# A retention layer with two feed-forward layers in float32: the gate in turns without a clamp pass, and the retention's decays moved from the output to query, state copy, key and mask

## The chip, the cores and the metric

The kernel runs as one program on one core of a Trainium2 chip. The metric is the device time of a run in microseconds. Three runs of the kernel before took 1521.79, 1521.57 and 1521.58 us; the median is 1521.58. The engines are named as in the profile: PE multiplies matrices into eight PSUM banks, DVE and ACT do elementwise work from and to SBUF and PSUM, POOL does elementwise work in SBUF, and SP does nothing here but issue DMAs. Each engine takes its instructions in the order in which the program hands them over, and waits where an operand is not there yet.

## The reference, cut to what matters

```python
gamma = 1.0 - 2.0 ** (-5.0 - np.arange(H))            # one per head, 8 heads
rel = pos[:, None] - pos[None, :]                     # 576 positions
Dmat = np.where(rel >= 0, gamma[:, None, None] ** rel, 0.0)
x = ((q @ k.T) / sqrt(64) * Dmat) @ v                 # retention; q, k, v: (8, 8, 576, 64)
x = x.transpose(0, 2, 1, 3).reshape(4608, 512)
h = x @ w_in                                          # 512 -> 2048
g = h * np.cos(h)                                     # the gate
x = g @ w_out                                         # 2048 -> 512
h = max(x @ w1, x @ w2, x @ w3)                       # 512 -> 768, three times
out = h @ w_out2                                      # 768 -> 512
```

## The kernel before

**Tiling and products.** The 4608 tokens are nine blocks of 512. Every matrix product is computed in 2x2 quarters by a scheme with seven products in place of eight, and each number is held as a high and a low part, so that one product is three matmuls per slice: low weight by high operand, high by high, high by low. `x_x`, `x_y`, `x_z` and `x_g` are such operands (high parts made by ACT, L360, low parts by DVE, L364), `w_wi` and so on the weights.

**Phases.** From about 0 to 80 us a lead-in splits the first weights and runs the first retention units. From 80 to about 375 us, phase A, the products by two of the four weight groups of w_in run for all blocks, between the retention's matmuls. From there to 573 us, phase B, the other two groups run on operands that are loaded again from DRAM. Then follow the phases wo (w_out), b (w1, w2, w3) and o (w_out2).

**The retention.** One unit is one block and one pair of heads: 36 units. A unit's load brings query, key transposed, key and value into one tile `u` (one DMA, L486). POOL scales the values by gamma to the minus position (`att_scale`, L492). PE computes scores (L504) into two banks `sc`, DVE multiplies them by a causal mask of ones and zeros on the way to SBUF (L513). A running state in PSUM takes key times value per chunk (L547); ACT copies it (L531) ahead of each chunk that follows. PE sums scores by values and query by the state copy into a bank `po` (L563, L575). DVE evacuates `po` chunk by chunk, by a column factor and a row factor (`att_decay`, L590), into the quarters `k_x` from which the operands of the first layer are made. A unit has four chunks of 128 tokens, or three and two of 64.

**The gate.** `group_in` (L405) makes the seven products of one weight group for one block into banks d, b and a; ACT copies and DVE adds (L410) evacuate them into `s_a`. The half tiles of 128x1024 then go through `gate` (L443): ACT takes the number of turns (s over 2 pi plus a quarter, as an integer, L448), DVE subtracts it (rest, L452), a clamp bounds the rest (L453; on POOL in phase A, on DVE in phase B), ACT takes the cosine (L457), DVE multiplies (times, L460), and SP stores the half in DRAM for phase wo (L466).

**What sets the order.** The order is written out by an agenda: `at(n, fn)` puts a piece of work n slots ahead, and `tick()`, called after every product (12 matmuls), hands over what is due. In `gate` the steps stand at `first`, `first + 1`, `first + gap` and so on, `gap` is 3. In `att_unit` the scores stand at `start`, the masks at `start + 1`, the output at `start + 5`, the decay at `start + 6`. All DMAs are issued by SP in one order, so that a store that waits for its gate holds back the loads behind it. Tiles come from a pool of 22 of 4 KB per partition and eight of 14 KB.

Of the kernel before, what the change touches and what calls it, by code (L numbers as in the profile page):

```python
# [20 lines left out]
NB = 512  # L21
# [12 lines left out]
HALF_PI = math.pi / 2.0  # L34
R_LEAST = -0.75
R_MOST = 0.25
WSCALE = 256.0
# [64 lines left out]
def retention_ffn(ctx: ExitStack, tc: tile.TileContext, att, w_in, w_out, w123, w_out2, cst, out):  # L102
# [293 lines left out]
    def last_product(own_slot=True):  # L396

        g = pending.pop()
        product_in(g["d"], g["ws"], P_A22, g["xs"], False)
        nc.scalar.copy(g["s1"][:, 0], g["d"][:, : g["n"]])  # L400
        g["done"](g, 1)
        if own_slot:
            tick()

    def group_in(ws, xs, name, done, where):  # L405
        n = HB * len(ws)
        g = {"ws": ws, "xs": xs, "name": name, "n": n, "done": done, "at": where}
# [9 lines left out]
        s0 = g["s0"] = x4(f"s0_{name}", [2, n])  # L417
        nc.scalar.copy(s0[:, 0], d[:, :n])  # L418
# [4 lines left out]
        nc.scalar.copy(s1[:, 1], b[:, :n])  # L423
        tick()
# [17 lines left out]

    def gate(s, name, dst, first, gap, eng):  # L443
# [75 lines left out]

    def att_keep(n, i):  # L520
# [57 lines left out]

    def att_decay(n):
        u = units.pop(n)  # L580
        j, hp = order_of(n)
        o = quarters_of.setdefault(j, {"name": f"x{j}", "n": NB})
        half = f"k{hp // 2 + 1}"
        if half not in o:
            o[half] = x4(f"{half}_x{j}", [2, NB])
        for _, m, c, pos in chunks_of(j):
            t, cc = divmod(c, HB)
            g = CGS + hp * 9 + pos // 64
            at_ = (hp % 2) * HB + cc
            nc.vector.scalar_tensor_tensor(  # L590
                out=o[half][:, t, at_ : at_ + m],
                in0=u["po"][:, c : c + m],
                scalar=cs[:, g : g + 1],
                in1=cs[:, CG + hp * CH : CG + hp * CH + m],
                op0=ALU.mult,
                op1=ALU.mult,
            )

    def att_unit(n, start):

        at(max(0, start - 1), lambda: att_scale(n))
        at(start, lambda: att_scores(n))
        at(start, lambda: att_keep(n, 0))
# [323 lines left out]
    for j in range(NBLK):  # L927
        for k, ids in enumerate(B_GROUPS):
# [65 lines left out]
```

## Time and profile before

| | |
|---|---|
| median of three runs | 1521.58 us |
| span of the profiled execution | 1516.2 us |
| PE busy | 1454.9 us, 96% |
| DVE busy | 1224.6 us, 81%, 1759 instructions |
| ACT busy | 726.8 us, 48%, 1214 instructions |
| POOL busy | 268.7 us, 18%, 216 instructions |
| moved by DMA | 324 MB, mean 214 GB/s |

A profile is one execution. Its span ends earlier than the measured time begins and ends, by 5.4 us against the median. The busy shares are means over stages that differ; the rows below cut the span by stage.

### The profile page before, as it was taken

To read this page: it belongs to the slowest core of one execution; us is meant where nothing else is said; L and a number is where in the kernel's file an instruction comes from. 1 tells how busy PE (TensorE), PEld (TensorE's weight loads), DVE (VectorE), ACT (ScalarE), POOL (GpSimd) and SP (SyncE) were. 2 spreads that over 40 slices of the span, in tenths; PEclk is the share of its full clock that TensorE was granted. 3 is DMA by queue.
4 is the path that set the end of the run, shared out by engine and by line. 5 is a ranking of instruction groups with operands and counts; after the bars stand their busy time and mean duration, and the time that the engine had idled before them with its cause. 6 is when DMAs were issued, how large, how long until landed. Compare 5 with 4: busy or idle time off the path is not lost.

```text
span 1516.2 us, 30767 instructions
## 1 busy us (share of the span) xinstructions
PE 1454.9 (96%) x12506; PEld 1416.0 (93%) x12506; DVE 1224.6 (81%) x1759; ACT 726.8 (48%) x1214; POOL 268.7 (18%) x216
## 2 busy tenths in 40 slices
PE   6899999999899997899999999999999999999998
PEld 5798989998889997899999999999999999999998
DVE  6888999989889989999999998656664555538997
ACT  3555555556667755454445444334432333323332
POOL 3344444444222001100000000000000000004221
PEclk9899999999999998999999999999999999999999
DMA  7588888876989984556555568923431110254443
GB/s 292 181 292 304 309 300 301 318 290 240 355 304 364 328 294 156 184 193 215 193 203 195 196 216 323 397 107 119 147 127 48 70 66 34 70 191 163 168 168 138
DMA packets 83084, 324.46 MB, mean 214 GB/s; under 512 B 9216, under 2 KB 9216, under 8 KB 76928
## 3 DMA queue, kind: packets, MB, share of 16 engines
q1 hardware_dynamic: 82944, 322.51, 59.4%
q8 instruction: 98, 1.61, 0.4%
q14 instruction: 42, 0.34, 0.1%
HBM read 190.35 MB, written 132.12 MB: 213 GB/s over the span
## 4 chain that ended last, share of the span: by engine, by line
PE 46%; DVE 6%; issue 3%; DMA 2%; ACT 1%; POOL 0%; DVEq 0%; SPq 0%; ACTq 0%; POOLq 0%
PE wo L795 17%; PE d_b L385 14%; PE b_b L385 7%; PE o L795 4%; PE a_b L385 3%; DVE l_m L768 1%; DMA st_o<-p_o 1%; DVE tb_m L356 1%; DVE o_o L808 1%; DVE x_m L759 1%; DVE u_o L808 1%; DMA raw_b<-w 1%; DVE l_g L768 0%; DMA k_m<-mq 0%; ACT h_m L763 0%
## 5 line engine op out<-in xcount | busy, mean ns | idle before, releaser
L795 PE MATMUL wo<-h_g,w_wo 128*128 128x256 f32 x1728 | 314.9, 284 | 0.0
L795 PEld LDWEIGHTS wo<-h_g,w_wo 128*128 128x128 f32 x1728 | 271.3, 193 | 0.0
L795 PE MATMUL wo<-l_g,w_wo 128*128 128x256 f32 x864 | 246.6, 285 | 7.6 <-DVE l_g L768 7.6
L385 PE MATMUL d_b<-x_z,w_b 128*128 128x256 f32 x1944 | 248.8, 283 | 2.9 <-ACT s_b L430 2.1
L385 PEld LDWEIGHTS d_b<-x_z,w_b 128*128 128x128 f32 x1944 | 239.9, 192 | 3.7 <-ACT s_b L430 2.7
L795 PEld LDWEIGHTS wo<-l_g,w_wo 128*128 128x128 f32 x864 | 166.7, 193 | 9.6 <-DVE l_g L768 9.5
L385 PE MATMUL b_b<-x_z,w_b 128*128 128x256 f32 x972 | 131.6, 283 | 2.0 <-DVE x_z L364 2.0
L385 PE MATMUL d_a<-x_x,w_wi 128*128 128x256 f32 x864 | 123.2, 293 | 4.1 <-DVE x_x L364 2.9
L385 PEld LDWEIGHTS b_b<-x_z,w_b 128*128 128x128 f32 x972 | 123.2, 192 | 2.2 <-DVE x_z L364 2.2
L385 PE MATMUL d_a<-x_y,w_wi 128*128 128x256 f32 x864 | 115.3, 291 | 9.2 <-ACT s_a L418 5.8
L385 PEld LDWEIGHTS d_a<-x_y,w_wi 128*128 128x128 f32 x864 | 110.9, 199 | 10.4 <-ACT s_a L418 6.5
L385 PEld LDWEIGHTS d_a<-x_x,w_wi 128*128 128x128 f32 x864 | 110.2, 195 | 8.9 <-DVE x_x L364 4.1
L795 PE MATMUL o<-h_m,w_o 128*128 128x256 f32 x648 | 117.5, 283 | 0.0
L763 ACT CAST h_g<-tb_g 128x1024 fp32r<-128x1024 f32 x36 | 37.8, 1051 | 150.5 <-DVE tb_g L356 145.9
L795 PEld LDWEIGHTS o<-h_m,w_o 128*128 128x128 f32 x648 | 101.1, 192 | 0.0
L452 DVE SCALAR_TENSOR_TENSOR t_a<-s_a,t_a 128x1024 f32<-128x1024 f32 x72 | 99.8, 1389 | 1.4 <-ACT t_a L448 1.4
L410 DVE TENSOR_TENSOR s_b<-s_b,b_b 128x512 f32<-128x512 f32 (+1 forms) x45 | 28.5, 634 | 87.1 <-PE b_b L385 87.0
L460 DVE TENSOR_TENSOR s_a<-s_a,t_a 128x1024 f32<-128x1024 f32 x72 | 90.6, 1274 | 5.9 <-ACT t_a L457 5.9
L457 ACT ACTIVATE t_a<-t_a 128x1024 f32<-128x1024 f32 x72 | 76.3, 1062 | 34.8 <-DVE t_a L453 25.6
L410 DVE TENSOR_TENSOR s_b<-s_b,a_b 128x512 f32<-128x512 f32 (+1 forms) x45 | 28.5, 634 | 79.2 <-PE a_b L385 69.4
L795 PE MATMUL o<-l_m,w_o 128*128 128x256 f32 x324 | 91.8, 283 | 0.0
L418 ACT COPY s_b<-d_b 128x512 f32<-128x512 f32 (+1 forms) x45 | 24.5, 544 | 127.3 <-PE d_b L385 120.0
(173 smaller groups left out, 3003.1 us busy)
## 6 DMA issues: line engine op xcount, KB each, us to landing
u<-att SPq DMA_DIRECT2D x36, 1024.0 KB, 7.3
gq<-s_a SPq DMA_DIRECT2D x72, 512.0 KB, 6.4
k_g<-gq SPq DMA_DIRECT2D x72, 512.0 KB, 6.6
xs<-x_x SPq DMA_DIRECT2D x63, 512.0 KB, 7.3
x_y<-xs SPq DMA_DIRECT2D x63, 512.0 KB, 7.9
w_b<-st_b SPq DMA_DIRECT2D x8, 1792.0 KB, 13.0
st_b<-p_b SPq DMA_DIRECT2D x27, 512.0 KB, 3.8
raw_b<-w SPq DMA_DIRECT2D x18, 512.0 KB, 6.1
```

The costliest lines, as they stand in the source:

```text
L356: eng.tensor_tensor(out=d, in0=a, in1=b, op=ALU.subtract)
L385: nc.tensor.matmul(h[:, p * HB : (p + 1) * HB], a, b, start=first and p == 0 and i == 0, stop=i == len(terms) - 1, skip_group_check=True,)
L410: nc.vector.tensor_tensor(out=dst, in0=dst, in1=b[:, :n], op=ALU.add)
L418: nc.scalar.copy(s0[:, 0], d[:, :n])
L452: nc.vector.scalar_tensor_tensor(out=r, in0=s, scalar=INV2PI, in1=st["t"], op0=ALU.mult, op1=ALU.subtract)
L457: nc.scalar.activation(r, r, AF.Sin, scale=TURN, bias=HALF_PI)
L460: nc.vector.tensor_tensor(out=s, in0=s, in1=f32(st["t"]), op=ALU.mult)
L759: nc.vector.tensor_tensor(out=o["x"][:, 1], in0=o["k1"][:, 0], in1=f32(o["x"][:, 0]), op=ALU.subtract)
L763: nc.scalar.copy(h, o[pairs[k][2]])
L768: nc.vector.tensor_tensor(out=lo, in0=o[pairs[k][2]], in1=f32(h), op=ALU.subtract)
L795: nc.tensor.matmul(b[:, mt * HB : (mt + 1) * HB], a, v, start=first and mt == 0 and p == 0 and i == 0, stop=last and p == len(ws) - 1 and ...
L808: nc.vector.scalar_tensor_tensor(out=d, in0=b, scalar=scale, in1=other, op0=ALU.mult, op1=ALU.add)
```

## The change

Two parts. **The gate in turns.** The evacuations of the w_in products carry the factor 1/(2 pi), so that `s_a` holds turns; ACT's first pass adds a quarter and makes an integer, the rest pass takes the smaller of s and 2^31 before it subtracts, the multiplication takes the larger of the cosine and -1. The clamp pass is gone; the cosine, the multiplication and the store stand one slot earlier; the factor 2 pi goes into the scale of phase wo. **The decays.** DVE multiplies the query in place by the row factors (`att_queries`, a slot ahead of the scores); the mask takes a factor per partition, a column of the constants; the state copy takes the chunk's factor as its scale; POOL scales the key for the state in place of the value; and `po` is evacuated by one copy on ACT (`att_evacuate`).

```diff
-    def group_in(ws, xs, name, done, where):
+    def group_in(ws, xs, name, done, where, scale):
...
-            nc.vector.tensor_tensor(out=dst, in0=dst, in1=b[:, :n], op=ALU.add)
+            nc.vector.scalar_tensor_tensor(out=dst, in0=b[:, :n], scalar=scale, in1=dst, op0=ALU.mult, op1=ALU.add)
+
+        def copy(dst, b):
+            nc.scalar.activation(dst, b[:, :n], AF.Copy, scale=scale)
...
-            nc.scalar.activation(st["t"], s, AF.Copy, scale=INV2PI, bias=0.25)
+            nc.scalar.activation(st["t"], s, AF.Copy, bias=0.25)
...
-            nc.vector.scalar_tensor_tensor(out=r, in0=s, scalar=INV2PI, in1=st["t"], op0=ALU.mult, op1=ALU.subtract)
-            eng.tensor_scalar(out=r, in0=r, scalar1=R_MOST, scalar2=R_LEAST, op0=ALU.min, op1=ALU.max)
+            nc.vector.scalar_tensor_tensor(out=r, in0=s, scalar=MOST_TURNS, in1=st["t"], op0=ALU.min, op1=ALU.subtract)
...
-            nc.vector.tensor_tensor(out=s, in0=s, in1=f32(st["t"]), op=ALU.mult)
+            nc.vector.scalar_tensor_tensor(out=s, in0=f32(st["t"]), scalar=-1.0, in1=s, op0=ALU.max, op1=ALU.mult)
...
-        at(first + gap, cosine)
-        at(first + gap + 1, times)
-        at(first + gap + 3, lambda: nc.sync.dma_start(out=dst, in_=s))
+        at(first + 2, cosine)
+        at(first + 3, times)
+        at(first + 5, lambda: nc.sync.dma_start(out=dst, in_=s))
...
-        v = units[n]["kv"][:, 1].rearrange("p (s d) -> p s d", d=64)
+        kn = units[n]["kv"][:, 0].rearrange("p (s d) -> p s d", d=64)
...
+    def att_queries(n):
+        qT = units[n]["qk"][:, 0]
+        j, hp = order_of(n)
+        nfull = sum(m == CH for _, m, _, _ in chunks_of(j))
+        for at_, k, w in ((0, nfull, CH), (nfull * CH, 2 * (NB // CH - nfull), CH // 2)):
+            if k:
+                q = qT[:, at_ : at_ + k * w].rearrange("p (s i) -> p s i", i=w)
+                col = CG + hp * CH
+                nc.vector.tensor_tensor(
+                    out=q, in0=q, in1=cs[:, col : col + w].unsqueeze(1).to_broadcast([128, k, w]), op=ALU.mult
+                )
...
-                    nc.vector.tensor_tensor(
+                    g = row + 2 * hp + e
+                    nc.vector.scalar_tensor_tensor(
...
+                        scalar=cs[:, g : g + 1],
...
-            nc.scalar.copy(um, st)
+            g = CGS + hp * 9 + pos // 64
+            nc.scalar.activation(um, st, AF.Copy, scale=cs[:, g : g + 1])
...
-    def att_decay(n):
+    def att_evacuate(n):
...
-        for _, m, c, pos in chunks_of(j):
-            t, cc = divmod(c, HB)
-            g = CGS + hp * 9 + pos // 64
-            at_ = (hp % 2) * HB + cc
-            nc.vector.scalar_tensor_tensor(
-                out=o[half][:, t, at_ : at_ + m],
-                in0=u["po"][:, c : c + m],
-                scalar=cs[:, g : g + 1],
-                in1=cs[:, CG + hp * CH : CG + hp * CH + m],
-                op0=ALU.mult,
-                op1=ALU.mult,
-            )
+        at_ = (hp % 2) * HB
+        nc.scalar.copy(o[half][:, :, at_ : at_ + HB], u["po"].rearrange("p (t c) -> p t c", c=HB))
...
         at(max(0, start - 1), lambda: att_scale(n))
+        at(max(0, start - 1), lambda: att_queries(n))
...
-        late = (1 if half else 2, 3, nc.vector) if k > 1 else (1, 3, nc.gpsimd)
+        first = 1 if half or k < 2 else 2
```

How the instructions move shows in three places, all on DVE. The first is its start. Before, after the state's bank is cleared, it joins the first weights' halves (`t_wi`, `raw_wi`) and masks unit 0's scores (`u` from `sc`):

```order
L618 MEMSET state 128x512
L176 TENSOR_SCALAR t_wi_187<-t_wi_187 128x512
L177 SCALAR_TENSOR_TENSOR raw_wi_0_173<-raw_wi_0_173,t_wi_187 128x512
L176 TENSOR_SCALAR t_wi_187<-t_wi_187 128x512
L177 SCALAR_TENSOR_TENSOR raw_wi_1_174<-raw_wi_1_174,t_wi_187 128x512
L513 TENSOR_TENSOR u_0_177<-sc_0_193,cs 128x512
L513 TENSOR_TENSOR u_0_177<-sc_1_194,cs 128x512
```

After, unit 0's query stands ahead of the joins, and unit 1's behind the masks:

```order
L631 MEMSET state 128x512
L509 TENSOR_TENSOR u_0_177<-u_0_177,cs 128x512
L179 TENSOR_SCALAR t_wi_187<-t_wi_187 128x512
L180 SCALAR_TENSOR_TENSOR raw_wi_0_173<-raw_wi_0_173,t_wi_187 128x512
L179 TENSOR_SCALAR t_wi_187<-t_wi_187 128x512
L180 SCALAR_TENSOR_TENSOR raw_wi_1_174<-raw_wi_1_174,t_wi_187 128x512
L532 SCALAR_TENSOR_TENSOR u_0_177<-sc_0_194,cs 128x512
L532 SCALAR_TENSOR_TENSOR u_0_177<-sc_1_195,cs 128x512
L509 TENSOR_TENSOR u_1_179<-u_1_179,cs 128x512
```

The query was not there before, and the joins have moved behind it; they now wait for what it waits for, the load of unit 0.

The second is a stretch of phase A, at the scores of the second unit of block 3 (`u_1`); `po` is the output of a unit of block 2, `s_a` and `t_a` the gate's tiles. Before:

```order
L410 TENSOR_TENSOR s_a_1_1182<-s_a_1_1182,b_a_1_1206 128x512
L590 SCALAR_TENSOR_TENSOR k_x_1221<-po_1302,cs 128x128 x4
L410 TENSOR_TENSOR s_a_1_1219<-s_a_1_1219,d_a_1_1169 128x512
L452 SCALAR_TENSOR_TENSOR t_a_0_1_1345<-s_a_0_995,t_a_0_1_1345 128x1024
L513 TENSOR_TENSOR u_1_1259<-sc_0_1362,cs 128x384
L513 TENSOR_TENSOR u_1_1259<-sc_0_1362,cs 128x128
L513 TENSOR_TENSOR u_1_1259<-sc_1_1363,cs 128x384
L513 TENSOR_TENSOR u_1_1259<-sc_1_1363,cs 128x128
L364 TENSOR_TENSOR x_x_1_1375<-k_x_1221,x_x_1_1375 128x512
L452 SCALAR_TENSOR_TENSOR t_a_1_0_1379<-s_a_1_1182,t_a_1_0_1379 128x1024
```

After:

```order
L413 SCALAR_TENSOR_TENSOR s_a_1_1160<-b_a_1_1184,s_a_1_1160 128x512
L509 TENSOR_TENSOR u_1_1237<-u_1_1237,cs 128x384
L509 TENSOR_TENSOR u_1_1237<-u_1_1237,cs 128x128
L413 SCALAR_TENSOR_TENSOR s_a_1_1197<-d_a_1_1147,s_a_1_1197 128x512
L458 SCALAR_TENSOR_TENSOR t_a_0_1_1320<-s_a_0_979,t_a_0_1_1320 128x1024
L532 SCALAR_TENSOR_TENSOR u_1_1237<-sc_0_1337,cs 128x384
L532 SCALAR_TENSOR_TENSOR u_1_1237<-sc_0_1337,cs 128x128
L532 SCALAR_TENSOR_TENSOR u_1_1237<-sc_1_1338,cs 128x384
L532 SCALAR_TENSOR_TENSOR u_1_1237<-sc_1_1338,cs 128x128
L367 TENSOR_TENSOR x_x_1_1350<-k_x_1199,x_x_1_1350 128x512
```

Where the four decays out of `po` stood, there are now the two parts of the query of the unit whose scores follow; the masks have become SCALAR_TENSOR_TENSOR, in the same place.

The third is one group in phase B; `s_a_2` and `s_a_3` are halves of its weight groups 2 and 3, `t_a` the gate's second tile. Before:

```order
L452 SCALAR_TENSOR_TENSOR t_a_2_1_5611<-s_a_2_5416,t_a_2_1_5611 128x1024
L453 TENSOR_SCALAR t_a_2_1_5611<-t_a_2_1_5611 128x1024
L452 SCALAR_TENSOR_TENSOR t_a_3_0_5646<-s_a_3_5519,t_a_3_0_5646 128x1024
L453 TENSOR_SCALAR t_a_3_0_5646<-t_a_3_0_5646 128x1024
L410 TENSOR_TENSOR s_a_2_5644<-s_a_2_5644,a_a_2_5668 128x512
L460 TENSOR_TENSOR s_a_2_5416<-s_a_2_5416,t_a_2_1_5611 128x1024
L460 TENSOR_TENSOR s_a_3_5519<-s_a_3_5519,t_a_3_0_5646 128x1024
L410 TENSOR_TENSOR s_a_2_5644<-s_a_2_5644,b_a_2_5648 128x512
L410 TENSOR_TENSOR s_a_2_5661<-s_a_2_5661,d_a_2_5631 128x512
```

After:

```order
L458 SCALAR_TENSOR_TENSOR t_a_2_1_5487<-s_a_2_5295,t_a_2_1_5487 128x1024
L465 SCALAR_TENSOR_TENSOR s_a_2_5295<-t_a_2_1_5487,s_a_2_5295 128x1024
L458 SCALAR_TENSOR_TENSOR t_a_3_0_5521<-s_a_3_5395,t_a_3_0_5521 128x1024
L413 SCALAR_TENSOR_TENSOR s_a_2_5518<-a_a_2_5542,s_a_2_5518 128x512
L465 SCALAR_TENSOR_TENSOR s_a_3_5395<-t_a_3_0_5521,s_a_3_5395 128x1024
L413 SCALAR_TENSOR_TENSOR s_a_2_5518<-b_a_2_5523,s_a_2_5518 128x512
L413 SCALAR_TENSOR_TENSOR s_a_2_5536<-d_a_2_5505,s_a_2_5536 128x512
```

The multiplication `s_a_2<-s_a_2,t_a_2` stood behind two rest passes, two clamps and an add; it now follows the rest pass of its own tile, with nothing between them.

## Rows read from the trace of the kernel before

**Rows 1.** Stretches by stage: width; PE, PEld, DVE, ACT, POOL busy (count); PEclk, DMA share, GB/s.
```profile
0.00:80.00 80.00, 60.10 (x520) 49.47 (x522) 62.65 (x119) 35.22 (x82) 29.06 (x28) 0.94 0.63 238
80.00:350.00 270.00, 266.04 (x2724) 243.81 (x2721) 243.88 (x388) 162.06 (x324) 117.09 (x97) 1.00 0.84 297
350.00:390.00 40.00, 33.45 (x260) 32.67 (x259) 36.24 (x49) 26.89 (x42) 18.43 (x12) 0.96 0.82 307
390.00:573.00 183.00, 177.05 (x1437) 176.11 (x1435) 166.49 (x211) 122.23 (x172) 24.42 (x16) 0.97 0.89 324
573.00:640.00 67.00, 53.94 (x390) 51.20 (x388) 65.48 (x87) 35.90 (x53) 10.41 (x6) 0.92 0.47 157
sum 1516.20, PE 1454.89 PEld 1416.05 DVE 1224.56 ACT 726.80 POOL 268.66; mean PE 242.48 PEld 236.01 DVE 204.09 ACT 121.13 POOL 44.78
```

**Rows 2.** PE's waits from 0 to 80 us: waited for, total us, times, longest us.
```profile
PE state L547 <- ACT u L531: 7.0, 12, 2.0
```

**Rows 3.** Groups by form, DVE: line, op, out<-in, shapes, count; busy us, mean ns; idle before.
```profile
L590 DVE SCALAR_TENSOR_TENSOR k_x<-po,cs 128x128 f32<-128x128 f32 x128 | 36.8, 342 | 1.4 <-PE po L575 1.4
L453 DVE TENSOR_SCALAR t_a<-t_a 128x1024 f32<-128x1024 f32 x36 | 30.8, 855 | 1.2
L364 DVE TENSOR_TENSOR x_z<-k_z,x_z 128x512 fp32r<-128x512 f32 x27 | 18.5, 687 | 3.3 <-ACT x_z L360 3.3
L513 DVE TENSOR_TENSOR u<-sc,cs 128x128 f32<-128x128 f32 x32 | 8.9, 277 | 0.0
```

**Rows 4.** Groups by form, ACT, the columns of rows 3.
```profile
L457 ACT ACTIVATE t_a<-t_a 128x1024 f32<-128x1024 f32 x72 | 76.3, 1062 | 34.8 <-DVE t_a L453 25.6 <-POOL t_a L453 9.1
L418 ACT COPY s_a<-d_a 128x512 f32<-128x512 f32 x36 | 20.9, 580 | 30.8 <-PE d_a L385 28.2 <-DMA x_y<-xs 2.6
```

**Rows 5.** Groups by form, POOL.
```profile
L453 POOL TENSOR_SCALAR t_a<-t_a 128x1024 f32<-128x1024 f32 x36 | 40.2, 1117 | 61.2 <-DVE t_a L452 52.6 <-DMA x_y<-xs 6.3 <-DMA u<-att 2.3
```

**Rows 6.** Timeline of PE, lead-in: start us, duration us, instruction, count, idle before.
```profile
45.01 1.16 PE L504 MATMUL sc<-u 64*128 64x128 f32 x16
```

**Rows 7.** Timeline of DVE, lead-in, the columns of rows 6.
```profile
50.12 0.69 DVE L364 TENSOR_TENSOR x_x<-tb_x,x_x 128x512 fp32r<-128x512 f32 x1
```

**Rows 8.** Timeline of DVE in phase A, at unit 9's scores.
```profile
88.34 1.24 DVE L590 SCALAR_TENSOR_TENSOR k_x<-po,cs 128x64 f32<-128x64 f32 x5
93.21 1.79 DVE L364 TENSOR_TENSOR x_x<-k_x,x_x 128x512 fp32r<-128x512 f32 x1
```

**Rows 9.** Timeline of POOL in phase A.
```profile
93.18 1.27 POOL L356 TENSOR_TENSOR ta_x<-k_x,k_x 128x512 f32<-128x512 f32 x1
```

**Rows 10.** Timeline of PE in phase A: unit 9's scores.
```profile
89.51 1.16 PE L504 MATMUL sc<-u 64*128 64x128 f32 x16
```

**Rows 11.** PE's waits from 350 to 390 us, the columns of rows 2.
```profile
PE d_a L385 <- DMA x_y<-xs: 3.3, 1, 3.3
PE d_a L385 <- DVE x_x L364: 2.0, 1, 2.0
PE d_a L385 <- ACT s_a L430: 1.0, 1, 1.0
```

**Rows 12.** Timeline of DVE at the end of phase A.
```profile
355.38 2.06 DVE L452 SCALAR_TENSOR_TENSOR t_a<-s_a,t_a 128x1024 f32<-128x1024 f32 x1
```

**Rows 13.** Timeline of DVE in phase B.
```profile
438.67 0.42 DVE L190 TENSOR_TENSOR s_wo<-fa_wo 128x256 f32<-128x256 f32 x1 [4.08 <-DMA fa_wo<-wf_wo]
496.41 1.21 DVE L452 SCALAR_TENSOR_TENSOR t_a<-s_a,t_a 128x1024 f32<-128x1024 f32 x1
497.65 0.69 DVE L453 TENSOR_SCALAR t_a<-t_a 128x1024 f32<-128x1024 f32 x1
500.72 2.36 DVE L460 TENSOR_TENSOR s_a<-s_a,t_a 128x1024 f32<-128x1024 f32 x2
504.19 1.22 DVE L452 SCALAR_TENSOR_TENSOR t_a<-s_a,t_a 128x1024 f32<-128x1024 f32 x1
```

**Rows 14.** PE's waits from 573 to 640 us, the columns of rows 2.
```profile
PE wo L795 <- DVE l_g L768: 7.0, 6, 1.9
```

More of the change, by code (lines that the diff above doesn't have):

```diff
@@ L34 @@
 HALF_PI = math.pi / 2.0
-R_LEAST = -0.75
-R_MOST = 0.25
+MOST_TURNS = 2.0**31
 WSCALE = 256.0
@@ L69 @@
 CTV = CGS + NPAIR * 9
-NCONST = CTV + NBLK * NPAIR * 8
+CKV = CTV + NBLK * NPAIR * 8
+NCONST = CKV + 2 * H
 def constants():
@@ L82, in constants @@
     c[:, CM2 : CM2 + CH] = c[:, CM : CM + CH] * ((np.arange(CH) // 64)[None, :] == (p // 64)[:, None])
+    for h in range(H):
+        c[:, CKV + h] = gamma[h] ** -p.astype(np.float64)
+        c[:, CKV + H + h] = gamma[h] ** -(p % 64).astype(np.float64)
     for j in range(NBLK):
@@ L399, in last_product @@
         product_in(g["d"], g["ws"], P_A22, g["xs"], False)
-        nc.scalar.copy(g["s1"][:, 0], g["d"][:, : g["n"]])
+        nc.scalar.activation(g["s1"][:, 0], g["d"][:, : g["n"]], AF.Copy, scale=g["scale"])
         g["done"](g, 1)
@@ L403, in last_product @@
             tick()
-    def group_in(ws, xs, name, done, where):
+    def group_in(ws, xs, name, done, where, scale):
         n = HB * len(ws)
-        g = {"ws": ws, "xs": xs, "name": name, "n": n, "done": done, "at": where}
+        g = {"ws": ws, "xs": xs, "name": name, "n": n, "done": done, "at": where, "scale": scale}
         def plus(dst, b):
-            nc.vector.tensor_tensor(out=dst, in0=dst, in1=b[:, :n], op=ALU.add)
+            nc.vector.scalar_tensor_tensor(out=dst, in0=b[:, :n], scalar=scale, in1=dst, op0=ALU.mult, op1=ALU.add)
+        def copy(dst, b):
+            nc.scalar.activation(dst, b[:, :n], AF.Copy, scale=scale)
         def go(b, product, first):
@@ L417, in group_in @@
         s0 = g["s0"] = x4(f"s0_{name}", [2, n])
-        nc.scalar.copy(s0[:, 0], d[:, :n])
+        copy(s0[:, 0], d)
         tick()
@@ L422, in group_in @@
         s1 = g["s1"] = x4(f"s1_{name}", [2, n])
-        nc.scalar.copy(s1[:, 1], b[:, :n])
+        copy(s1[:, 1], b)
         tick()
@@ L429, in group_in @@
         go(d, P_S2, False)
-        nc.scalar.copy(s0[:, 1], d[:, :n])
+        copy(s0[:, 1], d)
         tick()
@@ L441, in group_in, with gate @@
         pending.append(g)
-    def gate(s, name, dst, first, gap, eng):
+    def gate(s, name, dst, first):
         st = {}
@@ L609, in att_unit @@
         at(start + 5, lambda: att_out(n))
-        at(start + 6, lambda: att_decay(n))
+        at(start + 6, lambda: att_evacuate(n))
     NUNIT = NBLK * NPAIR
@@ L738, in gate_half @@
         j, k = g["at"]
-        late = (1 if half else 2, 3, nc.vector) if k > 1 else (1, 3, nc.gpsimd)
-        gate(g["s0"] if half == 0 else g["s1"], f"{g['name']}_{half}", gq[j][k][:, 2 * half : 2 * half + 2], *late)
+        first = 1 if half or k < 2 else 2
+        gate(g["s0"] if half == 0 else g["s1"], f"{g['name']}_{half}", gq[j][k][:, 2 * half : 2 * half + 2], first)
     OUT_ORDER = (P_A11, P_A12, P_S4, P_S2, P_A22, P_S3, P_S1)
@@ L865, in retention_ffn @@
                     (j, k),
+                    INV2PI,
                 )
@@ L890, in retention_ffn @@
     at(28 * (NBLK - 1) + 21, lambda: block_in(0, 0, 2, 3))
-    phase_out("wo", [[2 * k, 2 * k + 1] for k in range(4)], todo, lambda j, k: outs.pop((j, k)), WSCALE**-2, x2q)
+    phase_out("wo", [[2 * k, 2 * k + 1] for k in range(4)], todo, lambda j, k: outs.pop((j, k)), TURN * WSCALE**-2, x2q)
     take("b", 8)
@@ L936, in retention_ffn @@
                 outs[0, 0] = build_out("m0_0", NB, mq[0][0], range(1, 7), -0)
-            group_in([weights["b", i] for i in ids], later_y[j], f"b{j}_{k}", branch_half, (j, k))
+            group_in([weights["b", i] for i in ids], later_y[j], f"b{j}_{k}", branch_half, (j, k), 1.0)
     todo = [(j, k) for j in range(NBLK) for k in range(2)]
```

10 lines of the change are left out of this document (6 added, 4 removed).

## The prediction

> **What bounds the kernel now.** I read the table of stretches first: it splits the span into stages, and in each the width less PE's busy time is what PE stood idle. The lead-in (0 to 80 us) shows 19.9 us, phase A with the retention (80 to 350) 4.0, the passage to phase B (350 to 390) 6.6, phase B (390 to 573) 6.0, the start of phase wo (573 to 640) 13.1 [rows 1]. So phase A is bound by PE, and the other four hold what the change can win. The granted clock, below 1.00 there, adds a second account: 0.96 of 40 us, 0.97 of 183 and 0.92 of 67 are some 1.6, 5.5 and 5.4 us of full-speed time lost [rows 1]. After 640 us no gate and no retention unit is left.
>
> Then I read the waits, stage by stage. The lead-in waits for ACT's state copies [rows 2]. The passage waits for a DMA, for DVE's low parts and for an ACT copy [rows 11]. The wo start waits for DVE [rows 14], busy 65.48 of 67 us there and 166.49 of 183 in phase B [rows 1]. Last I read single instructions, to price what moves.
>
> The profiled execution has a span of 1516.2 us [rows 1]; the median is 1521.58, so 5.4 us lie outside the span. My sum is made on the span, and the 5.4 are added.
>
> **The change part by part.** *The clamp.* 36 passes leave DVE (mean 855 ns, 30.8 us [rows 3]), 36 leave POOL (mean 1117 ns [rows 5]). Nothing replaces them: the bound goes into passes that are there, as a second operation. The multiplication becomes a SCALAR_TENSOR_TENSOR of 128x1024 with two SBUF inputs; the rest pass has that form already and takes 1.21 us, the multiplication 2.36 for two [rows 13], so 0 for the new form. Evacuations with a scale instead of a plain copy: 0 to 0.01 us each, hidden under the next product.
>
> *Its schedule.* The cosine and the multiplication stand one slot earlier. ACT sat idle 34.8 us before cosines, 25.6 for DVE's clamp and 9.1 for POOL's [rows 4]. But less stands between the rest pass and the multiplication. In phase B, where DVE is behind, its row before is rest, clamp, rest, clamp, add, two multiplications, two adds: 7.78 us from one rest pass (496.41) to its like (504.19) [rows 13]. After, DVE goes from the rest pass straight to the multiplication of the same tile, and waits there for ACT's cosine, 1.06 us [rows 4] and the hand-overs, some 1.2; behind it stand the next rest pass and the adds that evacuate PE's banks, and PE waits for those. The other half has one add of 0.6 us between: some 0.6 of waiting. Where DVE is behind, two clamps (2 x 0.69, [rows 13]) are thus paid for by 1.8 us of waiting: nothing gained, 0.4 per group lost. Where DVE keeps up, the wait falls into time that it would idle anyway.
>
> *The decays.* 128 decays of 342 ns [rows 3] and 32 of half their width leave DVE. In their place a unit has one evacuation by ACT (580 ns by the copy of 128x512 [rows 4]; ACT has room, 162 of 270 us in phase A [rows 1]), and DVE multiplies the query in place (one pass per unit, in two parts where a unit has half-width chunks, 52 in 36 units): 128x512 from SBUF, 0.69 us by the nearest row [rows 3], and up to 1.79 by a row of the same shape beside POOL [rows 8]. The masks take a pointer scalar: 65 ns more by the two 128x128 rows (342 against 277, [rows 3]), 104 times, 6.8 us in all. The state copy as ACTIVATE: 0 to 0.02 us each. Per unit DVE gives back four or five decays (1.24 us for five in a row, [rows 8]) and takes 0.7 to 1.8 for the query and 0.2 for masks: -0.3 to +0.8.
>
> *The new wait.* Scores now wait for DVE's query; before they waited for their load alone. The order puts the query where the earlier unit's decays stood. In phase A DVE came there at 88.34 and the scores began at 89.51 [rows 8, 10]: 1.17 us of room, enough for 0.69, not for 1.79. In the lead-in the room is negative: for unit 5 DVE reaches the query's place at about 50.1, the scores began at 45.01 [rows 6, 7].
>
> The contended figure is one row: a DVE pass with two SBUF inputs at 93.21 took 1.79 while POOL's subtraction ran from 93.18 for 1.27 [rows 8, 9]. The Trainium skill ("SBUF — State Buffer", Who interferes with whom) states the rule: a DVE operation with two SBUF inputs and a GpSimd one that reads SBUF exclude each other, while a DVE operation with one SBUF input is spared. By that rule the change trades spared passes (decays out of PSUM) for queries that can be shut out, and the first rival below is what it would then cost; that row agrees.
>
> **The sum, by stage.** Lead-in: DVE loses some 9 us of decays of eight units and takes 6 of queries and 1.5 of masks, a gain of 1.5; against it unit 5's scores (and 6's) come some 3 us later, part of which PE would have waited anyway for the state (7.0 us in 12 waits, [rows 2]). I take +1 (-3 to +5). Phase A: bound by PE; of the 4.0 us idle -0.5, queries fit: -0.5 (-2 to +4). Passage: the low part that PE waited 2.0 for stands behind rest passes of 2.06 us [rows 12] against 1.21 alone; without POOL's clamp beside them that wait and ACT's 1.0 go, while the 3.3 of a DMA [rows 11] stay. With the clock: -3 (-8 to 0). Phase B: most PE loss comes where DVE waited 4.08 us for a weight load [rows 13] that SP issues behind a store of a gated tile; one slot earlier (1.44 us) the store frees SP earlier: -2 (-8 to +6; the upper end if DVE's waits reach PE, 18 groups x 0.4, the lower if stalls and half the clock's loss go). Start of wo: four clamps of 0.69 out, four cosine waits of 0.6 to 1.2 in: -0.5 (-4 to +3). Rest: 0. Sum -5: span 1511.2, and 1516.6 with the 5.4, so 1516.5. Ends of single terms don't all meet; 1507 to 1526 holds most.
>
> **Rivals.** *Scores wait for the query all through phase A* (slower). POOL's scaling of k starts on the same landing as the query, and its subtractions run beside. If a query takes 1.79, it ends 0.6 us after the scores' time; for 28 units that is 17 us, less the 4.5 won elsewhere: about 1534. It decides from 1.17 us per query. Against it: POOL is busy only 117 of 270 us [rows 1].
>
> *The clamp's time turns into the wait for the cosine* (about no change, to slower). Then phase B and wo gain nothing (+0.4 x 18 = 7 at the worst), the passage gives -3, the lead-in +1: 1519.5 to 1526, say 1523. For it: the order puts rest pass and multiplication side by side. Against: 16.5 us of idle DVE in phase B that can take it.
>
> *The passes come back one for one* (faster). If the 25.7 us that PE stood idle from 350 to 640 [rows 1] mostly hung on DVE's clamps (30.8 us), 20 go and with +1 the time is about 1502. Against it: the DMA share is 0.89 in phase B, and 3.3 us of the passage waited for DMA.
>
> *It does nothing that counts*: transfers pace 350 to 573 anyway, lead-in takes back the rest: 1521.
>
> **How the numbers follow.** Forecast 0.52 (its own range 1511 to 1521); scores waiting 0.12; the wait in place of the clamp 0.18; one for one 0.12; nothing that counts 0.06. A measurement here tells 0.2%, 3.0 us, from no change: faster is below 1518.5, slower above 1524.6. The forecast gives 0.40 faster and 0.12 same; one for one 0.12 faster; the wait for the cosine 0.02 faster, 0.09 same, 0.07 slower; nothing that counts 0.05 same, 0.01 slower; scores 0.12 slower. In all 0.54, 0.26, 0.20. The range leaves out 1534 and 1502, and the thin ends.
>
> **What would show it.** In the profile after: no POOL pass of 128x1024, POOL's busy time down by some 40 us and DVE's by some 45 (30.8 and 45 of decays out; some 25 of queries and 7 of masks in). PE's waits should name the query's line for the lead-in only, for at most 5 us; 28 such waits of 0.6 us would prove the first rival. DVE's multiplication should show idle time ended by ACT's cosine: below 15 us my forecast stands, above 30, with PE's loss in phase B unchanged or up, the second rival. The passage should lose its 2.0 and 1.0 us waits. The prediction is wrong if the lead-in grows by more than 5 us, or if phase B is longer than 183 us.

## The result, and the profile after

The changed kernel took 1529.33 us in the median against 1521.57 of the kernel before on the same chips: ratio 1.0055, 95% interval [1.0040, 1.0069]. It is slower by some 8 us where the prediction said 5 us faster, and outside its range. The profiled execution has a span of 1525.5 us against 1516.2, 9.3 us more. One per cent is 15.2 us in what follows.

PE's program is the same in all these kernels, so the start of one and the same matmul tells how far each lies behind. Read from the timelines, unit 9's scores begin at 89.51 before [rows 10] and at 96.19 after (+6.7); the first product on an operand that was loaded again (`x_y`, the start of phase B) at 377.37 and 384.06 (+6.7); the first matmul of phase wo at 573.24 and 584.71 (+11.5); the first of phase b at 958.52 and 967.98 (+9.5). So the loss has two places: the lead-in, and phase B. The stretches of the kernel after, by the same cuts as [rows 1]:

```profile
0.00:80.00 80.00, 53.99 (x453) 45.09 (x454) 61.34 (x98) 38.64 (x81) 26.36 (x25) 0.91 0.57 215
80.00:350.00 270.00, 264.01 (x2706) 241.45 (x2706) 221.09 (x299) 180.85 (x348) 93.21 (x70) 1.00 0.87 300
350.00:390.00 40.00, 35.93 (x306) 34.57 (x306) 34.28 (x47) 30.55 (x49) 9.17 (x6) 1.00 0.72 271
390.00:573.00 183.00, 171.38 (x1396) 169.03 (x1395) 142.57 (x172) 121.28 (x172) 24.53 (x15) 0.99 0.91 326
573.00:640.00 67.00, 54.61 (x415) 52.31 (x415) 63.86 (x88) 39.13 (x57) 9.57 (x6) 0.95 0.45 156
```

PE is 6.1 us less busy in the lead-in and 5.7 less from 390 to 573. The passage and the start of wo are shifted by 7 to 11 us in this table, so their rows can't be compared one by one. DVE is busy 23.9 us less in the 183 us, and PE is none the better for it. PE's waits of the kernel after, lead-in first (0 to 80 us), then phase B (390 to 573):

```profile
PE sc L521 <- issue: 8.7, 2, 5.2
PE sc L521 <- DVE u L509: 6.7, 2, 4.3
...
PE d_a L388 <- ACT s_a L416: 6.6, 7, 1.6
PE d_a L388 <- DMA x_y<-xs: 3.0, 2, 1.8
PE b_a L388 <- ACT s_a L416: 2.5, 1, 2.5
```

The line of the scores appears with 15.4 us in four waits; "issue" is what the profile shows where it can't name the releaser, and the timelines below name it: the query. In phase B the waits for ACT's copies went from 5.8 us in three to 9.1 in eight; those of the kernel before:

```profile
PE d_a L385 <- ACT s_a L418: 5.8, 3, 3.7
```

Where DVE stood, and what the first instructions of the lead-in took, from DVE's timeline after:

```profile
10.23 0.69 DVE L509 TENSOR_TENSOR u<-u,cs 128x512 f32<-128x512 f32 x1 [2.91 <-DMA u<-att]
10.84 1.26 DVE L179 TENSOR_SCALAR t_wi<-t_wi 128x512 uint32<-128x512 uint32 x1
12.75 1.28 DVE L179 TENSOR_SCALAR t_wi<-t_wi 128x512 uint32<-128x512 uint32 x1
14.07 1.41 DVE L180 SCALAR_TENSOR_TENSOR raw_wi<-raw_wi,t_wi 128x512 uint32<-128x512 uint32 x1
...
45.81 0.69 DVE L367 TENSOR_TENSOR x_x<-ta_x,x_x 128x512 fp32r<-128x512 f32 x1 [2.72 <-ACT x_x L363]
...
55.03 1.83 DVE L509 TENSOR_TENSOR u<-u,cs 128x384 f32<-128x384 f32 x2
```

from POOL's, beside the joins:

```profile
10.28 1.55 POOL L497 TENSOR_TENSOR u<-u,cs 128x512 f32<-128x512 f32 x1 [9.83 <-DMA u<-att]
12.71 1.04 POOL L497 TENSOR_TENSOR u<-u,cs 128x512 f32<-128x512 f32 x1 [0.89 <-DMA u<-att]
13.71 1.22 POOL L186 TENSOR_TENSOR fa_wi<-raw_wi 128x512 uint32<-128x512 uint32 x1
```

from PE's:

```profile
48.84 1.69 PE L388 MATMUL d_a<-x_x,w_wi 128*128 128x256 f32 x12
55.68 2.08 PE L521 MATMUL sc<-u 64*128 64x128 f32 x16 [5.15 <-issue]
```

and the first and the last of the four joins on DVE before:

```profile
7.27 0.41 DVE L176 TENSOR_SCALAR t_wi<-t_wi 128x512 uint32<-128x512 uint32 x1
8.78 0.69 DVE L177 SCALAR_TENSOR_TENSOR raw_wi<-raw_wi,t_wi 128x512 uint32<-128x512 uint32 x1
```

Unit 0's query waits for its load and ends at 10.9; the four joins, which ended by 9.5 before, now follow it, beside POOL, and three of the four take 1.26 to 1.41 us in place of 0.41 to 0.69. Unit 5's scores, at 45.01 before [rows 6], begin at 55.68, when the first part of the query given to DVE at 55.03 is there; PE stood for 5.15 us. The groups by form, first of DVE:

```profile
L458 DVE SCALAR_TENSOR_TENSOR t_a<-s_a,t_a 128x1024 f32<-128x1024 f32 x72 | 100.9, 1404 | 0.0
L465 DVE SCALAR_TENSOR_TENSOR s_a<-t_a,s_a 128x1024 f32<-128x1024 f32 x72 | 89.5, 1242 | 24.8 <-ACT t_a L462 24.7
L509 DVE TENSOR_TENSOR u<-u,cs 128x512 f32<-128x512 f32 x20 | 16.1, 803 | 4.0 <-DMA u<-att 4.0
L532 DVE SCALAR_TENSOR_TENSOR u<-sc,cs 128x128 f32<-128x128 f32 x32 | 10.7, 336 | 0.0
```

and of ACT:

```profile
L462 ACT ACTIVATE t_a<-t_a 128x1024 f32<-128x1024 f32 x72 | 76.1, 1057 | 42.4 <-DVE t_a L458 42.4
L609 ACT COPY k_x<-po 128x512 f32<-128x512 f32 x36 | 20.9, 581 | 3.7 <-PE po L597 3.7
L553 ACT ACTIVATE u<-state,cs 128x128 f32<-128x128 f32 x128 | 45.7, 369 | 80.5 <-PE state L569 80.4
```

Two groups of the kernel before, the multiplication and the state copy:

```profile
L460 DVE TENSOR_TENSOR s_a<-s_a,t_a 128x1024 f32<-128x1024 f32 x72 | 90.6, 1274 | 5.9 <-ACT t_a L457 5.9
L531 ACT COPY u<-state 128x128 f32<-128x128 f32 x128 | 32.4, 265 | 93.1 <-PE state L547 92.9
```

The prices of the prediction held for the most part: query 803 ns (0.69 to 1.79 foretold), mask 336 against 277 (+59, foretold 65), evacuation 581 (580), DVE's multiplication no dearer in its new form. One did not: the state copy with a factor per partition takes 369 ns where the plain copy took 265, not 0 to 0.02 us more. The idle times at the right are the ones to look at: DVE stood 24.8 us before multiplications (5.9 in the kernel before), ACT 42.4 before cosines (34.8, [rows 4]), although the clamp that ACT had waited for is gone.

### The profile page after: what moved, and what is told of

Its sections match the earlier page's. It is cut to its first block, busy times and chain, and to the rows that moved or that the text cites. A ratio compares the mean times of both kernels' runs of the same rounds, so it can differ in the third digit from the quotient of the medians.

```text
span 1525.5 us, 30471 instructions
## 1 busy us (share of the span) xinstructions
PE 1451.9 (95%) x12506; PEld 1411.8 (93%) x12506; DVE 1181.2 (77%) x1615; ACT 758.0 (50%) x1250; POOL 231.0 (15%) x180
## 4 chain that ended last, share of the span: by engine, by line
PE 43%; DVE 7%; DMA 4%; issue 2%; ACT 1%; SPq 0%; POOL 0%; DVEq 0%; ACTq 0%; POOLq 0%
PE wo L808 15%; PE d_b L388 14%; PE b_b L388 7%; PE o L808 4%; PE a_b L388 3%; DVE l_m L781 1%; DMA st_o<-p_o 1%; DVE tb_m L359 1%; DMA k_z<-x2q 1%; DMA k_g<-gq 1%; DVE o_o L821 1%; DMA raw_b<-w 1%; DVE l_g L781 1%; DVE x_m L772 1%; DVE u_o L821 0%
## 5 line engine op out<-in xcount | busy, mean ns | idle before, releaser
L416 ACT ACTIVATE s_b<-d_b 128x512 f32<-128x512 f32 (+1 forms) x90 | 49.9, 554 | 195.3 <-PE d_b L388 188.1
L388 PE MATMUL d_a<-x_y,w_wi 128*128 128x256 f32 x864 | 111.1, 284 | 12.0 <-ACT s_a L416 8.4
L388 PE MATMUL d_a<-x_x,w_wi 128*128 128x256 f32 x864 | 119.9, 289 | 1.8 <-DVE x_x L367 1.5
L388 PEld LDWEIGHTS d_a<-x_y,w_wi 128*128 128x128 f32 x864 | 106.3, 192 | 14.4 <-ACT s_a L416 11.4
L465 DVE SCALAR_TENSOR_TENSOR s_a<-t_a,s_a 128x1024 f32<-128x1024 f32 x72 | 89.5, 1242 | 24.8 <-ACT t_a L462 24.7
L462 ACT ACTIVATE t_a<-t_a 128x1024 f32<-128x1024 f32 x72 | 76.1, 1057 | 42.4 <-DVE t_a L458 42.4
L413 DVE SCALAR_TENSOR_TENSOR s_b<-b_b,s_b 128x512 f32<-128x512 f32 (+1 forms) x45 | 28.7, 637 | 86.9 <-PE b_b L388 86.9
L413 DVE SCALAR_TENSOR_TENSOR s_b<-a_b,s_b 128x512 f32<-128x512 f32 (+1 forms) x45 | 28.6, 637 | 79.2 <-PE a_b L388 69.3
```

Of the source, the lines that this page charges most:

```text
L388: nc.tensor.matmul(h[:, p * HB : (p + 1) * HB], a, b, start=first and p == 0 and i == 0, stop=i == len(terms) - 1, skip_group_check=True,)
L413: nc.vector.scalar_tensor_tensor(out=dst, in0=b[:, :n], scalar=scale, in1=dst, op0=ALU.mult, op1=ALU.add)
L416: nc.scalar.activation(dst, b[:, :n], AF.Copy, scale=scale)
L465: nc.vector.scalar_tensor_tensor(out=s, in0=f32(st["t"]), scalar=-1.0, in1=s, op0=ALU.max, op1=ALU.mult)
```

## The experiments

Theory A: the queries in the lead-in cost some 7 us, the gate is about even. Rival B: the slots into which cosine and multiplication moved are too early, and DVE's or ACT's waiting goes on to PE. Twelve kernels were run; each ratio is to the kernel before on the same chip. The last columns are starts of the same matmuls: unit 9's scores, the first product on `x_y`, the first of wo.

| kernel | ratio [95%] | u9 | x_y | wo |
|---|---|---|---|---|
| before | 1 | 89.5 | 377.4 | 573.2 |
| both (the change) | 1.0055 [1.0040, 1.0069] | 96.2 | 384.1 | 584.7 |
| 1 gate alone | 1.0039 [1.0027, 1.0052] | 86.8 | 380.2 | 584.3 |
| 2 retention alone | 1.0058 [1.0041, 1.0076] | 96.8 | 388.0 | 584.0 |
| 3 gate alone, old slots | 0.9913 [0.9884, 0.9942] | 87.1 | 373.0 | 563.6 |
| 4 both, units 0-7 old form | 1.0022 [1.0012, 1.0032] | 90.3 | 378.9 | 580.1 |
| 5 gate, only the cosine early | 0.9974 [0.9962, 0.9986] | 86.8 | 373.3 | 570.6 |
| 6 gate, early in phase A only | 0.9963 [0.9950, 0.9976] | 89.3 | 382.1 | 571.8 |
| 7 both, no queries in units 0-7 | 1.0021 [1.0009, 1.0032] | 89.8 | 377.9 | 582.0 |
| 8 as 4, old slots | 0.9923 [0.9902, 0.9943] | 91.0 | 378.1 | 568.6 |
| 9 both, old slots | 0.9978 [0.9968, 0.9988] | 95.2 | 382.1 | 573.0 |
| 10 clamp kept, early slots | 1.0182 [1.0164, 1.0200] | 89.7 | 382.7 | 603.3 |
| 11 gate, one slot later | 0.9954 [0.9938, 0.9969] | 88.7 | 374.3 | 572.5 |
| 12 as 8, plain state copy | 0.9915 [0.9902, 0.9929] | 89.2 | 375.3 | 566.8 |

**1. The gate alone.** The kernel before, with the change's edits of gate and scale alone.

> The gate part alone: no clamp pass, cosine, multiplication and store one slot earlier; the retention as before. Theory A (the retention's queries cost some 7 us in the lead-in, the gate part is about even): 1518 to 1522 us, PE's delay at 80 us against the kernel before within 0.5 us. Rival B (the multiplication now waits for ACT's cosine, and DVE passes that wait on to PE in phase B): 1524 to 1529, and the multiplication's idle time on DVE ended by ACT above 30 us.

1526.42 us: rival B, and not A. Yet multiplications waited 23.4 us for ACT, not the 30 of rival B: size missed, sign right.

**2. The retention alone.** The rest of the change.

> The retention part alone: query, state copy, key and mask carry the decays, ACT evacuates the output; the gate with its clamp as before. Theory A: 1526 to 1530 us, PE 6 to 7 us late at 80 us, and little more after. Rival B: 1520 to 1523, the loss of both changes together comes from the gate.

1530.27 us, just above A's range: 7.3 us late at unit 9, and 3.4 more by the start of phase B. By the ratios this part costs 0.58%, the gate 0.39, the two together 0.55, so they don't add up. The starts say where: from unit 9 to `x_y` the gate alone loses 5.5 us and the retention alone 3.4, but the two together none (287.9 us, as before). PE's waits for low parts from 80 to 350 us are 4.7 us in the gate alone, 0.9 in the retention alone and 0.2 in both; why, no run shows. What the gate alone loses in phase A can therefore not be put down to the change.

**3. The gate alone in the old slots.**

```diff
-        at(first + 2, cosine)
-        at(first + 3, times)
-        at(first + 5, lambda: nc.sync.dma_start(out=dst, in_=s))
+        at(first + 3, cosine)
+        at(first + 4, times)
+        at(first + 6, lambda: nc.sync.dma_start(out=dst, in_=s))
```

> The gate part alone without the clamp pass, but cosine, multiplication and store in the slots of before. Theory A: 1513 to 1519 us, since DVE gets 30.8 us back and the cosine is done when it comes to multiply. If the clamp's time on DVE was never on the path: within 1 us of the gate in earlier slots and of the kernel before.

1507.51 us, 13 below the kernel before and 19 below run 1, better than any theory had it. The clamp's time was on the path; the early slot spent all of it and 6 us more. ACT's cosines in the groups by form, of the gate alone:

```profile
L458 ACT ACTIVATE t_a<-t_a 128x1024 f32<-128x1024 f32 x72 | 76.1, 1056 | 47.2 <-DVE t_a L454 46.9
```

and of the gate in old slots:

```profile
L458 ACT ACTIVATE t_a<-t_a 128x1024 f32<-128x1024 f32 x72 | 76.2, 1058 | 7.8 <-DVE t_a L454 7.6
```

One slot, 12 matmuls or 1.44 us, makes 47.2 us of ACT's standing before cosines into 7.8, and DVE's 23.4 before multiplications into 9.8. What this does to PE, from `x_y` to wo, where PE's matmuls are the same; the gate alone first, then in old slots:

```profile
380.22:584.27 204.05, 189.46 (x1514) 186.53 (x1513) 158.68 (x196) 132.47 (x186) 25.19 (x16) 0.97 0.89 318
372.95:563.64 190.69, 184.26 (x1515) 183.09 (x1513) 154.42 (x197) 131.91 (x186) 26.37 (x16) 0.99 0.91 337
```

Of the 13.4 us, PE stood idle for 8.2 (14.6 against 6.4) and was busy 5.2 longer, at a mean granted clock of 0.97 against 0.99. How PE comes to stand shows in one group of phase B. The gate alone, DVE's timeline:

```profile
484.08 1.23 DVE L461 SCALAR_TENSOR_TENSOR s_a<-t_a,s_a 128x1024 f32<-128x1024 f32 x1 [1.12 <-ACT t_a L458]
485.22 1.22 DVE L454 SCALAR_TENSOR_TENSOR t_a<-s_a,t_a 128x1024 f32<-128x1024 f32 x1
```

ACT's:

```profile
486.47 1.06 ACT L458 ACTIVATE t_a<-t_a 128x1024 f32<-128x1024 f32 x1 [1.00 <-DVE t_a L454]
487.44 0.58 ACT L412 ACTIVATE s_a<-d_a 128x512 f32<-128x512 f32 x1
```

PE's:

```profile
488.07 1.10 PE L384 MATMUL d_a<-x_y,w_wi 128*128 128x256 f32 x7 [0.85 <-ACT s_a L412]
```

The gate in old slots, ACT's timeline at the same place of the next block:

```profile
486.57 1.05 ACT L458 ACTIVATE t_a<-t_a 128x1024 f32<-128x1024 f32 x1
488.96 0.60 ACT L412 ACTIVATE s_a<-d_a 128x512 f32<-128x512 f32 x1 [1.34 <-PE d_a L384]
489.45 1.05 ACT L458 ACTIVATE t_a<-t_a 128x1024 f32<-128x1024 f32 x1
```

In the early slots DVE waits 1.12 us for a cosine to multiply; the next rest pass stands behind that and ends at 486.44; ACT waits for it with the cosine, 1.00 us; and the copy out of bank d stands behind that cosine, so that PE, which needs the bank, waits 0.85. In the old slots the copy of d (488.96) is handed to ACT ahead of the cosine (489.45) and starts as PE ends. So the wait went round: ACT's cosine holds DVE, DVE's rest pass holds ACT, ACT's copy holds PE. The changed kernel shows the same: a cosine at 487.48 that waited 1.00 us, the copy behind it at 488.44, and PE's matmul at 489.07 after 0.85. One group doesn't price the loop; from 390 to 573 us PE's waits for ACT's copies are 9.8 us in eight in the gate alone and 3.6 in three in the old slots.

**4. Both, units 0 to 7 in the old form.** A test on the unit's number in `att_scale`, `att_queries`, `att_mask`, `att_keep` and `att_evacuate`.

> Both changes, but units 0 to 7 (the lead-in's) keep the old form: value scaled, plain state copy and mask, decays on the output; units 8 to 35 in the new form. Theory A: the 6.7 us at 80 us go, 1520 to 1523. Rival (the delay of the lead-in would be made up anyway, the loss sits in phases A and B): 1526 to 1529.

1523.42 us, 0.4 above A's range: unit 9's scores are at 90.3, so 5.9 of the 6.7 us of the lead-in are gone, of which 5 arrive at the end.

**5. Only the cosine early.** Multiplication and store in the old slots.

```diff
-        at(first + 3, times)
-        at(first + 5, lambda: nc.sync.dma_start(out=dst, in_=s))
+        at(first + 4, times)
+        at(first + 6, lambda: nc.sync.dma_start(out=dst, in_=s))
```

> The gate part alone, the cosine one slot early as in the change, multiplication and store in the slots of before. Theory D (the loss comes from DVE standing before the multiplication until the cosine is done): the loss goes, 1507 to 1511 us. Theory C (the loss comes from ACT standing before the cosine until DVE's rest pass is done, 47 us in the gate alone, with the copies that PE waits for queued behind the cosine): the loss stays, 1520 to 1527.

1517.59 us: in between, so each theory holds in part, and the starts say where. Until `x_y` the loss is gone (373.3, as in run 3): in phase A it was DVE standing before the multiplication (theory D), with the low parts that PE waits for behind it. Between `x_y` and wo run 3 took 190.7 us, run 5 197.3, run 1 204.1: in phase B each of the two accounts for half. The halves are rough, since the profiled execution (1513.38 us) is the fastest of ten and 4.2 us below their median. ACT still stood 35.4 us before cosines; DVE stood none before multiplications, but 26.1 before rest passes. PE's waits from 80 to 350 us, in the gate alone first:

```profile
PE d_a L384 <- DVE x_x L363: 4.7, 5, 1.3
PE state L548 <- ACT u L532: 3.6, 5, 0.7
```

and in this run, where the second is the only one:

```profile
PE state L548 <- ACT u L532: 3.6, 5, 0.7
```

SP has a share that these runs don't part from it: its waits for the gate's stores are 183.9 us in run 1, 127.0 in run 5, 101.0 in run 3, and the loads stand behind them.

**6. Early in phase A only.** An argument to `gate`: one slot later for k > 1.

> The gate part alone without a clamp, cosine, multiplication and store one slot early in phase A, in the slots of before in phase B. If the early slots cost in both phases, as PE's delays in the gate alone suggest (some 7 us until 373 us, some 10 after): 1513 to 1518 us. If only phase B, where DVE is behind, pays: 1507 to 1510. If only phase A: 1524 to 1527.

1516.01 us, as the first case had it: in the gate alone both phases pay.

**7. No queries in the lead-in.**

```diff
     def att_queries(n):
+        if n < 8:
+            return
```

> Both changes; units 0 to 7 leave out the multiplication of the query (their scores and outputs lack that factor), all else of the change is there, the evacuation on ACT too. Theory A (scores wait for the query's place in DVE's queue): PE's 6.7 us at 80 us go, 1521 to 1524 us. Rival (ACT's evacuations, in whose queue the high parts stand, make the lead-in late): 1526 to 1530.

1523.69 us, as run 4 within 0.3: theory A. ACT's evacuations cost the lead-in nothing that shows. The stretch to 80 us, PE busy second, of this run:

```profile
0.00:80.00 80.00, 61.01 (x516) 50.59 (x518) 58.62 (x90) 42.70 (x89) 28.94 (x27) 0.91 0.62 238
```

and of run 4:

```profile
0.00:80.00 80.00, 60.14 (x520) 49.37 (x522) 63.87 (x116) 37.57 (x84) 28.54 (x27) 0.94 0.64 239
```

PE's 54.0 us are 61.0 and 60.1, as the 60.1 before [rows 1].

**8. As run 4, in the old slots.**

> The retention in the new form from unit 8 on, the gate without a clamp in the slots of before. If the two losses are the only ones and the retention's part pays from unit 8 on: 1503 to 1507 us, below the gate in old slots alone. If the new form costs in phase A too (some 3 us there by PE's delay with both changes): 1509 to 1513.

1509.15 us: the second case. The new form wins nothing from unit 8 on, although DVE has less to do (225.6 us busy from 80 to 350 us against 232.8); 0.9923 and run 3's 0.9913 can't be told apart. Between unit 9 and `x_y` it takes 287.1 us against 285.9. Less than 2 us of one profile is not to be read, though: runs 1, 3, 5 and 6 share their lead-in's retention, and their unit 9 begins between 86.8 and 89.3.

**9. Both in the old slots.** The edit of run 3 on the changed kernel.

> Both changes as they are, only cosine, multiplication and store in the slots of before. If the early slots (some 17 to 19 us in the gate alone) and the lead-in's queries (some 6 us) are separate costs that add up: 1513 to 1517 us, 13 to 16 below both changes with early slots, and below the kernel before.

1516.59 us: as expected, and faster than the kernel before by 0.22% [0.12, 0.32]. The slot is worth 0.77% here, some 12 us, and most of it in phase B: from `x_y` to wo 190.8 us in place of 200.6, from unit 9 to `x_y` 286.9 in place of 287.9. The new form in the lead-in is worth 0.55% against run 8, and 0.33% in the early slots (run 4).

**10. The clamp kept, early slots.** In the kernel before the gap of 3 becomes 2.

> The kernel before with its clamp; only cosine, multiplication and store one slot earlier: the move of the slots by itself. If the early slot costs by the length of what must fit into it, it costs more with the clamp than without: 1535 to 1550 us. If it costs the same as without the clamp: 1535 to 1541. If the clamp filled the time in which the cosine is awaited: 1522 to 1530.

1549.03 us, the first case: 28 us for the slot with a clamp, 19 without. What the slot costs depends on what has to fit into it. ACT's cosines, by form:

```profile
L457 ACT ACTIVATE t_a<-t_a 128x1024 f32<-128x1024 f32 x72 | 76.3, 1060 | 83.7 <-DVE t_a L453 61.1 <-POOL t_a L453 22.3
```

and PE's longest entry from 390 to 573 us, 6.6 in both changes together:

```profile
PE d_a L385 <- ACT s_a L430: 16.4, 8, 2.6
```

**11. One slot later than before.** `first + 4`, `+ 5`, `+ 7`, without a clamp.

> The gate alone without a clamp, cosine, multiplication and store one slot later than before. If DVE and ACT are still waiting on each other in the old slots (7.8 us of ACT before cosines, 9.8 us of DVE before multiplications in that kernel): 1500 to 1506. If the old slots have room enough: 1506 to 1510, and above that if the tiles that are held longer hold up their successors.

1513.26 us, above run 3 by some 6: the last case in sign. The old slot is the best of three. The loss lies between `x_y` and wo (198.2 us against 190.7): PE waits there 5.5 us in six for ACT's copies (3.6 in three in run 3) and once 4.6 us for a load of `x_y` (2.7 in run 3). Whether tiles held longer cause that was not tried.

**12. As run 8, with plain state copies.**

```diff
-                nc.scalar.activation(um, st, AF.Copy, scale=cs[:, g : g + 1])
+                nc.scalar.copy(um, st)
```

> As the retention in the new form from unit 8 on with the gate in old slots (1509.15 us), but the state copies from unit 8 on are plain copies again; the output of those units lacks the chunk's factor on the state's share. The copy with a factor per partition takes 369 ns against 265, and stands between two state products of PE. Theory E (that is what the new form costs in phase A, where PE falls some 4 us behind from 86 to 291 us of the kernel before): the 4 us go, 1504 to 1507 us, PE at most 1 us behind at 291. Rival (scores and evacuations by ACT cost them): PE stays 3 to 4 us behind, 1508 to 1511.

1508.57 us against 1509.15, not to be told apart. From unit 9 to `x_y` it takes 286.1 us (run 8: 287.1; run 3: 285.9), differences too small to read from one profile. PE is 1.8 us behind at 291 us of the kernel before (run 8: 4.5, of which 1.5 already at unit 9), between the 1 of theory E and the 3 to 4 of its rival. So theory E is neither shown nor excluded; if it holds, it is worth 1 us at `x_y`. The copy takes 268 ns again, and the scores' waits from 80 to 350 us remain:

```profile
PE sc L526 <- PE state L585: 1.2, 2, 0.7
PE sc L526 <- DVE u L514: 0.8, 3, 0.3
PE sc L526 <- PE a_a L388: 0.5, 2, 0.3
```

With one of 0.2 they are 2.7 us in eight waits; run 3 has none. The profile puts 0.8 of them down to the query; all of them are a sixth of the first rival's 17 us.

## Why the prediction was wrong, step by step

The starts of the matmuls cut the 9.3 us of the span by place, against a forecast of -5: the lead-in +6.7 (forecast +1), phase A and the passage up to `x_y` 0.0 (-3.5), phase B +4.8 (-2), from wo on -2.2 (-0.5). Both signs of being wrong that the prediction named came true: the lead-in grew by more than 5 us, and phase B by 4.8.

**The step that failed most: the schedule's price in phase B.** The prediction saw that the multiplication would follow the rest pass of its own tile and wait for ACT, 1.2 and 0.6 us, and held that against the clamps: "0.4 per group lost", 7 us at the worst. Then it took -2, since idle DVE could take the wait and an earlier store would free SP. Clamp and slot can be read apart from `x_y` to wo: 195.9 us before, 190.8 without the clamp in the old slots (run 9), 200.6 in the change. So the clamp was worth 5 us there and the slot cost 9.8. What was left out is the third engine. The prediction read the 34.8 us that ACT stood before cosines as idle time to be won, and saw only DVE's rest pass and adds behind the wait; but ACT's cosine stands in front of a copy that frees a PE bank, and the earlier slot put it there. Nor did SP come free earlier: its waits for the gate's stores went from 116.7 to 172.3 us, and are 104.7 in run 9. The second rival had place, sign and, for phase B, the size right (4.8 of its 7 at the worst), and its chance of 0.18 was too low; its total of 1523 missed because it kept +1 for the lead-in and -3 for the passage. The 24.8 us of DVE before multiplications lie between the 15 and the 30 that were to decide; for ACT's standing before cosines, 42.4 us in the change and 7.7 in run 9, the text gave no bound.

**The clamp's value** was mis-sized the other way: in the gate alone, with its slots kept, it is 13 us (run 3); the prediction's terms for passage, phase B and wo were 5.5 in sum. That is about halfway to the 20 of the rival in which the passes come back one for one.

**The lead-in** was taken as +1 (-3 to +5) and measured +6.7. Unit 5's scores were put 3 us late and came 10.7 late. The price of the query was right; what failed was DVE's place. The room was short by 5.1 us by the prediction's own rows (50.1 against 45.01), and it counted on DVE being earlier by the decays; DVE came to the query at 55.03, 4.9 us later than its old timeline. Some of that is the joins behind the first query, beside POOL at twice to three times their time; but DVE stood 2.72 us for ACT until 45.81, so not all of it, and no run parts the rest. Run 7 takes the queries away, and all but 0.3 of the 6.7 us with them.

**Phase A**: -0.5 (-2 to +4) was forecast. Run 8 against run 3 shows the retention's new form from unit 8 on at 1.2 us to `x_y`, no gain in any case. The dearer state copy (104 ns more, priced at 0 to 20) can be 1 us of it. The early slots cost 0.9 us more in the change (against run 9; 1.5 by runs 4 and 8). They cost 7.5 in the gate alone (runs 1 and 3), where low parts of the next block stand behind the waiting multiplication. The first rival (28 waits of 0.6) fell: DVE is early enough in all but a few units.

**The passage**: PE's 2.0 us for the low part became 1.2 and the 1.0 of ACT went, most of what was forecast; but a wait of 1.4 us for a state copy stands there now, and from unit 9 to `x_y` nothing of the -3 is left.

**Luck:** run 9 ends at 1516.59 us, next to the forecast 1516.5, but with other terms: +5.7 in the lead-in, -0.9 up to `x_y`, -5.0 in phase B and -2.7 from wo on.

**What was forecast of the busy times** held and did not count: DVE's busy time fell by 43 us (45 forecast), POOL's by 38 (40).

## What to carry to other kernels

A pass that goes from a chain does not by itself allow the rest of the chain to stand earlier: whoever moves a step up in the order of an engine that serves PE should list what stands behind it on that engine, and what releases it. Take the pass away and leave the slots, then move one step at a time; here, in the gate alone, the first is 0.9913 [0.9884, 0.9942] of the time before, and each step moved up gives part of it back (runs 5 and 1). A factor that moves from an output to an input adds a wait before the first use, and here it cost most in the lead-in, where loads have just landed and the engine that applies it is behind: its units are better left in the old form (runs 4 and 8).

## What the runs showed of the hardware that was not expected

- An ACT copy of 128x128 out of PSUM with a factor per partition takes 369 ns (128 of them), a plain one 265 and, with a constant factor on an SBUF tile, 282. In the evacuations of 128x512 a constant factor changes 580 to 592.
- Three of DVE's first four joins in the lead-in took 1.26 to 1.41 us beside POOL's multiplication and sum where they took 0.41 to 0.69 alone, the TENSOR_SCALAR with one SBUF input among them (1.26 and 1.28 against 0.41 and 0.42). The Trainium skill ("SBUF — State Buffer", Who interferes with whom) lets TENSOR_SCALAR into the shared port pair where it can run in a two-port mode; these two rows agree.
